# Top-k attention and a mixture of depths on one core: the bound rounded by ScalarE, fillers of two tiles at once, the mixture in even pieces, and four unread bf16 products ahead of each first turning

## The chip, the cores and the metric

The kernel runs on one core of one Trainium2 chip. The metric is the time of one execution on the device, in microseconds. The engines are TensorE (PE in the profile, its weight loads PEld), VectorE (DVE), ScalarE (ACT), GpSimd (POOL) and SyncE (SP, which here only issues transfers). A difference of more than about 0.2% can be told from none.

## The reference

Batch 8, 8 heads, 576 tokens, head width 64, all in float32. Attention keeps the 32 largest scores of each row; then, per batch, 128 tokens of the 512-wide result go through a two-layer network of width 1024.

```python
scores = scale * np.matmul(q, k.transpose(0, 1, 3, 2))     # scale = 1/8
kth = np.partition(scores, -32, axis=-1)[..., -32:-31]
scores = np.where(scores >= kth, scores, -1e9)
attn = softmax(scores)
x = np.matmul(attn, v)             # (B,H,S,D) -> (B,S,H*D)
s = x @ w_gate                     # per batch
top_idx = np.argpartition(-s[b], 128)[:128]
ye = np.maximum(x[b, top_idx] @ w1, 0) @ w2
out[b, top_idx] = x[b, top_idx] + sigmoid(s[b, top_idx])[:, None] * ye
```

## The kernel before

Work is cut into units (batch b, row tile t, head pair hp). Row tiles t = 0 to 3 have 128 rows and give two score tiles of 128 x 576, one for each head; row tile 4 has 64 rows, and its two heads share one score tile. So a batch has 20 units, 16 of two tiles and 4 of one. A loop over n runs a pipeline in which one pass (a step) works on six units at once, and every engine's instructions stay in the order of the program text (`InOrder`):

- n+1: `multiply` makes the scores (tile ps) on TensorE; at the end of the step `keep` copies them to sc on ScalarE.
- n: `find_bound` on VectorE. Each row is cut into eight parts, the eight largest of each are candidates, and three rounds of maximum give the 24th largest candidate (tile best), a bound below which the 32nd largest score is near. `cut` writes it, rounded to bf16, to `seen[:, 0]`.
- n-1: `part` on ScalarE takes the Sign of each score against the bound (tile sides) and counts the signs in `seen[:, 2]`. `mask` on GpSimd multiplies the scores by the signs into y and appends eight columns of fillers, made from that count so that the eighth largest of y is the wanted 32nd score. `find_kth` on VectorE takes the eight largest (next8), and `lift` on GpSimd writes the eighth, times 2^90, to `seen[:, 1]`.
- n-2: Relu on ScalarE and a subtraction on GpSimd push all scores below the 32nd far down (tile z).
- n-3: `turn` and `turn_last` transpose z on TensorE (tiles ptr, last_ps), ScalarE takes the exponential (pT, last).
- n-4: `values` multiplies by v on TensorE (tile av), `keep_values` copies to xs. After the fourth head pair of a row tile, `normalise` divides on VectorE and GpSimd (tile x), and `gates` multiplies by w_gate on VectorE.

`mixture` is a generator; each step runs one piece of it, after a batch's last tile has its gates. Its ten pieces: two transposes of the gates, two of ranks on VectorE, the picks, the gather of picked tokens (xe_ps), a small product for row numbers and gates, two halves of the first layer (h_ps), and the second layer (y_ps), whose result gy goes out by a GpSimd transfer. `load_qkv` is a generator too: in steps 10 to 18 of a batch it loads and transposes the next batch's keys and queries and loads its values. Its transposes, the mixture and `turn_last` share one PSUM buffer (`ps_misc`); the turnings have two (`ps_tr`), the scores one set, the values one. Keys, queries and values have two buffers, the fetched rows three. The end of the program checks the assumptions behind the bound, and a general path stands behind that check; it is not run with this input.

In the profile nearly every instruction carries line 41, that of the helper that keeps the order, so groups are told apart by tile.

Of the kernel before, what the change touches and what calls it, by code (L numbers as in the profile page):

```python
# [9 lines left out]
AF = mybir.ActivationFunctionType  # L10
ALU = mybir.AluOpType
FP32 = mybir.dt.float32
# [7 lines left out]

BIG = 2.0**90

TALL = 2.0**20


LEAST = 1.0e-16
MOST = 1.0e6


# [15 lines left out]
def kernel(  # L45
# [21 lines left out]
    DE = D + 1  # L67
    NDC = HD // P
    NFC = F // P
    scale = 1.0 / float(D) ** 0.5  # L70
    assert D == 64 and R == 64 and HD == 512 and F % (4 * P) == 0
    assert moe_capacity == CAP and TOP_K % 8 == 0

# [16 lines left out]
    ident = const.tile([P, P], FP32, name="ident")  # L90
    make_identity(nc, ident)


    tok_i = const.tile([P, NT], I32, name="tok_i")
    nc.gpsimd.iota(tok_i[:, 0:J], pattern=[[1, J]], base=0, channel_multiplier=J)
# [12 lines left out]
    nc.gpsimd.memset(sums, 1.0)  # L108

    MIDDLE = S - 2 * (TOP_K - 8) + 1  # L110
    steps_i = const.tile([P, 8], I32, name="steps_i")
    nc.gpsimd.iota(steps_i, pattern=[[2, 8]], base=2 - MIDDLE, channel_multiplier=0)
    steps = const.tile([P, 8], FP32, name="steps")
    nc.vector.tensor_copy(out=steps, in_=steps_i)


# [40 lines left out]
        qT = kqpool.tile([P, NHP, S], FP32, name="qT")  # L157
        return kT, qT, vbufs[b % 2]

    def load_qkv(qb, kb, vb, kT, qT, vs):  # L160

        last = [ldpool.tile([R, H, D], FP32, name=f"last{i}", bufs=1) for i in range(2)]
        for rows, src in zip(last, (kb, qb)):
            nc.sync.dma_start(out=rows, in_=src[:, JP:S, :].rearrange("h p d -> p h d"))

        def fetch(i):
            hp, src = i // 2, (kb, qb)[i % 2]
            rows = ldpool.tile([P, J, 2, D], FP32, name="rows")
            for hh in range(2):
                nc.sync.dma_start(  # L170
                    out=rows[:, :, hh, :],
                    in_=src[2 * hp + hh, 0:JP, :].rearrange("(p j) d -> p j d", j=J),
                )
            return rows

        fetched = [fetch(i) for i in range(3)]
        vt, vlast, vpair = vs
        v_rows = vb[:, JP:S, :].rearrange("h p d -> p h d")
        nc.sync.dma_start(out=vlast[:, :, 0:D], in_=v_rows)
        for hh in range(2):  # L180
            nc.sync.dma_start(
                out=vpair[hh * R : (hh + 1) * R, :, hh, 0:D], in_=v_rows[:, hh::2, :]
            )
        tr = ps_misc.tile([P, 512], FP32, name="tr", tag="misc")
        for i in range(2 * NHP):
            w, hp = divmod(i, NHP)
            pe.transpose(
                tr[:, i * R : (i + 1) * R],
                last[w][:, 2 * hp : 2 * hp + 2, :].rearrange("p h d -> p (h d)"),
                ident[0:R, 0:R],  # L190
            )
        tails = tr.rearrange("p (w c r) -> p w c r", w=2, c=NHP)
        act.copy(out=kT[:, :, 0:R], in_=tails[:, 0, :, :])
        act.copy(out=kT[:, :, S : S + R], in_=tails[:, 0, :, :])
        act.copy(out=qT[:, :, JP:S], in_=tails[:, 1, :, :])
        yield
        for i in range(2 * NHP):
            tr = ps_misc.tile([P, 512], FP32, name="tr", tag="misc")
            for c in range(J):
                pe.transpose(  # L200
                    tr[:, c * P : (c + 1) * P],
                    fetched[i][:, c, :, :].rearrange("p h d -> p (h d)"),
                    ident,
                )
            if i % 2 == 0:
                act.copy(out=kT[:, i // 2, R:S], in_=tr)
            else:
                act.copy(out=qT[:, i // 2, 0:JP], in_=tr)
            if i + 3 < 2 * NHP:
                fetched.append(fetch(i + 3))  # L210
            nc.sync.dma_start(
                out=vt[:, i, :, 0:D],
                in_=vb[i, 0:JP, :].rearrange("(p j) d -> p j d", j=J),
            )
            yield

    def heads_of(t):

# [55 lines left out]

    def cut(n, best, at):

        pool.tensor_copy(
            out=seen[:, 0, at : at + n],
            in_=best.rearrange("p i e -> p (i e)").bitcast(BF16)[:, 15 : 16 * n : 16],
        )  # L280
# [13 lines left out]
            accum_out=seen[:, 2, at + i : at + i + 1],  # L294
        )

    def mask(i, sc, at, sides, y):

        pool.tensor_tensor(y[:, i, 0:S], sc[:, i, :], sides[:, i, :], ALU.mult)
        pool.tensor_scalar(  # L300
            out=y[:, i, S : S + 8],
            in0=steps,
            scalar1=seen[:, 2, at + i : at + i + 1],
            scalar2=-TALL,
            op0=ALU.add,
            op1=ALU.mult,
        )

    def find_kth(n, y):
# [9 lines left out]
    def turn(i, z):  # L319

        tr = ps_tr.tile([P, 512], FP32, name="ptr")
        for c in range(J):
            at = c * P + i * R
            pe.transpose(tr[:, c * P : (c + 1) * P], z[:, i, at : at + P], ident)
        return tr
# [135 lines left out]
    def mixture(row0, x, gate, rank, exact=False):  # L461
# [31 lines left out]
                    op0=ALU.is_equal,  # L493
                )

        yield
        ps = ps_misc.tile([P, 512], FP32, name="xe_ps", tag="misc")
        for dc in range(NDC):
            for t in range(NT):
                n = R if t == J else P  # L500
                pe.matmul(
                    ps[:, dc * CAP : (dc + 1) * CAP],
                    x[0:n, t, dc * P : (dc + 1) * P],
                    pick[0:n, t, :],
                    start=(t == 0),
                    stop=(t == J),
                )
        xeT = modpool.tile([P, NDC, CAP], FP32, name="xeT")
        act.copy(out=xeT, in_=ps.rearrange("p (c i) -> p c i", c=NDC))

        yield
        ps = ps_misc.tile([P, 512], FP32, name="extra_ps", tag="misc")
# [13 lines left out]
        dve.tensor_scalar_min(out=row_i, in0=picked[:, 0:1], scalar1=float(B * S - 1))  # L526

        hT = modpool.tile([P, NFC, CAP], FP32, name="hT")
        for f0 in range(0, NFC, 4):
            yield  # L530
            ps = ps_misc.tile([P, 512], FP32, name="h_ps", tag="misc")
            for i in range(4):
                for dc in range(NDC):
                    pe.matmul(
                        ps[:, i * CAP : (i + 1) * CAP],
                        w1[:, dc, (f0 + i) * P : (f0 + i + 1) * P],
                        xeT[:, dc, :],
                        start=(dc == 0),
                        stop=(dc == NDC - 1),
                    )  # L540
            act.activation(
                hT[:, f0 : f0 + 4, :], ps.rearrange("p (c i) -> p c i", c=4), AF.Relu
            )

        yield
        ps = ps_misc.tile([P, 512], FP32, name="y_ps", tag="misc")
        for fc in range(NFC):
            pe.matmul(
                ps, hT[:, fc, :], w2[:, fc, :], start=(fc == 0), stop=(fc == NFC - 1)
            )  # L550
        gy = modpool.tile([P, HD], FP32, name="gy")
        act.activation(gy, ps, AF.Copy, scale=picked[:, 1:2])

        nc.gpsimd.indirect_dma_start(
            out=out.flatten_outer_dims(),
# [29 lines left out]

    units = [(b, t, hp) for b in range(B) for t in range(NT) for hp in range(NHP)]
    per_batch = NT * NHP
    load_from = per_batch - 2 - 2 * NHP
    first_tile, tiles = [], 0
    for b, t, hp in units:  # L590
        first_tile.append(tiles)
        tiles += len(heads_of(t))
    qkv = {0: room_for_qkv(0)}
    loading = load_qkv(q[0], k[0], v[0], *qkv[0])
    next(loading)
    mixing = iter(())
    gating = normalising = None
    xs = x = gate = None
# [4 lines left out]

    for n in range(-1, len(units) + 6):
        if 0 <= n + 1 < NHP:
            next(loading)
            next(loading)
        if n == NHP:
            load_weights()

# [24 lines left out]
        if tiles_of(n - 1):  # L635
            sides = wkpool.tile([P, 2, S], BF16, name="sides")
            y = wkpool.tile([P, 2, S + 8], FP32, name="y")
            for i in range(tiles_of(n - 1)):
                part(i, scs[n - 1], first_tile[n - 1], sides)
                mask(i, scs[n - 1], first_tile[n - 1], sides, y)  # L640
            next8 = find_kth(tiles_of(n - 1), y)
        if tiles_of(n - 3):
            w = tiles_of(n - 3)
# [27 lines left out]
        if tiles_of(n - 4):  # L671
# [5 lines left out]
                    gate = xpool.tile([P, NT], FP32, name="gate")  # L677
            weights.pop(n - 4)
            keep_values(t, hp, av, xs)
        if gating is not None:  # L680
            b, t, *of_batch = gating
            gating = None
# [11 lines left out]
        if tiles_of(n - 4):  # L694
            b, t, hp = units[n - 4]
            if hp == NHP - 1:
                normalising = b, t, xs, x, gate
        if tiles_of(n):
            cut(tiles_of(n), bests.pop(n), first_tile[n])
        if tiles_of(n - 1):  # L700
            lift(tiles_of(n - 1), next8, first_tile[n - 1])
        b, i = divmod(n, per_batch)
        if n >= 0 and i >= load_from and b + 1 < B:
            if i == load_from:
                qkv[b + 1] = room_for_qkv(b + 1)
                loading = load_qkv(q[b + 1], k[b + 1], v[b + 1], *qkv[b + 1])
            next(loading, None)

    for _ in mixing:
        pass  # L710
# [4 lines left out]
    for what, op, than, limit in (  # L715
        (seen[:, 0, :], ALU.min, ALU.is_gt, LEAST),
        (seen[:, 1, :], ALU.min, ALU.is_gt, LEAST * BIG),
        (seen[:, 2, :], ALU.max, ALU.is_lt, float(MIDDLE)),
        (seen[:, 2, :], ALU.min, ALU.is_gt, float(MIDDLE - 16)),
        (sums.rearrange("p t h -> p (t h)"), ALU.max, ALU.is_lt, MOST),  # L720
    ):
        far = stats.tile([P, 1], FP32, name="far")
# [51 lines left out]
    def general(b, row0):  # L774
# [1 line left out]
            return a[bass.ds(b, 1)].rearrange("o a s d -> (o a) s d")  # L776

        kT, qT, vs = room_for_qkv(0)
        for _ in load_qkv(of(q), of(k), of(v), kT, qT, vs):
            pass  # L780
        x = xpool.tile([P, NT, HD], FP32, name="x")
        gate = xpool.tile([P, NT], FP32, name="gate")
        for t in range(NT):
# [64 lines left out]
```

## Time and profile before

| | |
|---|---|
| median of 3 runs | 1368.69 us (1368.59 to 1369.9) |
| profiled execution | 1366.38 us, of which the span is 1364.4 |
| granted TensorE clock, mean | 0.823 |
| busy: PE, PEld | 1111.4 us (81%), 885.7 (65%) |
| busy: DVE, ACT, POOL | 910.9 (67%), 853.6 (63%), 983.1 (72%) |
| DMA | 46.92 MB, 33 GB/s over the span |

The span runs from the first to the last instruction. The busy shares are averages over steps of different kinds; which engine ends last is read step by step. The granted clock is a share of full speed.

### The profile page before, as it was taken

How to read it: one execution, taken by the hardware profiler on the slowest of the kernel's cores; microseconds unless marked ns; L12 is line 12 of the kernel's file. 1: busy time of each engine (PE TensorE's matmuls, PEld its weight loads, DVE VectorE, ACT ScalarE, POOL GpSimd, SP SyncE). 2: the span in 40 equal slices, each digit the busy share in tenths (PEclk: the TensorE clock that was granted, in tenths of full speed). 3: DMA queues.
4: the chain of work that ended last, by engine and by line, in shares of the span. 5: the costliest groups of instructions: out<-in, count | busy, mean ns of one | idle time of the engine just before them, and what ended most of it. 6: DMA issues, size and time to landing. Idle time of an engine off the chain costs nothing. (4 is left out here: it accounts for less than half of the span.)

```text
span 1364.4 us, 23293 instructions
## 1 busy us (share of the span) xinstructions
PE 1111.4 (81%) x6938; PEld 885.7 (65%) x6938; DVE 910.9 (67%) x4978; ACT 853.6 (63%) x1921; POOL 983.1 (72%) x1254
## 2 busy tenths in 40 slices
PE   4778866987879879898788986788886988879867
PEld 2566645865668657686567765676665866658655
DVE  3777678657785587855777658864778647786440
ACT  3677676656665667565675576765666566666530
POOL 3888788677775777667786678865788567887730
PEclk9678888988678886888777888879858799779768
DMA  8501120113001120012200122001210010000000
GB/s 189 120 4 37 44 62 1 25 33 81 16 2 24 39 77 14 2 31 40 78 6 8 24 50 68 6 16 32 58 48 1 9 40 32 5 1 2 8 35 10
DMA packets 123189, 46.92 MB, mean 34 GB/s; under 512 B 118832, under 2 KB 118832, under 8 KB 122032
## 3 DMA queue, kind: packets, MB, share of 16 engines
q1 hardware_dynamic: 121904, 43.27, 13.0%
q0 software_dynamic: 1152, 2.10, 1.2%
q8 instruction: 57, 0.93, 0.3%
q14 instruction: 76, 0.62, 0.1%
HBM read 33.82 MB, written 11.53 MB: 33 GB/s over the span
## 5 line engine op out<-in xcount | busy, mean ns | idle before, releaser
L41 POOL TENSOR_TENSOR y<-sc,sides 128x576 f32<-128x576 f32 x288 | 368.8, 1281 | 226.6 <-ACT sides L41 216.3
L41 POOL TENSOR_TENSOR z<-sc,z 128x576 f32<-128x576 f32 x288 | 413.3, 1454 | 21.3 <-ACT z L41 10.2
L41 DVE MAX8 next<-y 128x8 f32<-128x584 f32 x288 | 219.5, 766 | 306.3 <-POOL y L41 305.7
L41 PE MATMUL av<-v,pT 128*128 128x65 f32 (+1 forms) x2560 | 379.8, 304 | 13.2 <-ACT xs L41 13.2
L41 PEld LDWEIGHTS av<-v,pT 128*128 128x128 f32 (+1 forms) x2560 | 362.1, 223 | 32.2 <-ACT xs L41 25.0
L41 DVE MAX8 cand<-sc 128x8 f32<-128x72 f32 x2304 | 324.0, 217 | 86.0 <-ACT sc L41 86.0
L41 PE MATMUL ptr<-ident,z 128*128 128x128 f32 x1152 | 227.7, 331 | 178.2 <-POOL z L41 177.7
L41 ACT ACTIVATE sides<-sc,seen 128x576 bf16<-128x576 f32 x288 | 221.6, 772 | 153.0 <-POOL seen L41 152.0
L41 PEld LDWEIGHTS ptr<-ident,z 128*128 128x128 f32 x1152 | 160.8, 174 | 233.9 <-POOL z L41 228.0
L41 PE MATMUL ps<-kT,qT 64*128 64x288 f32 (+1 forms) x1280 | 252.2, 524 | 2.7 <-ACT qT L41 2.7
L41 ACT COPY sc<-ps 128x576 f32<-128x576 f32 x288 | 171.7, 646 | 122.1 <-issue 91.7
L41 ACT ACTIVATE z<-sc,seen 128x576 f32<-128x576 f32 x288 | 209.3, 777 | 0.6 <-POOL seen L41 0.6
L41 ACT ACTIVATE pT<-ptr 128x512 f32<-128x512 f32 x288 | 158.5, 584 | 18.9 <-PE ptr L41 18.6
L41 PEld LDWEIGHTS ps<-kT,qT 64*128 64x128 f32 (+1 forms) x1280 | 128.2, 218 | 57.8 <-issue 13.7
L41 DVE MAX8 best<-cand 128x8 f32<-128x64 f32 x864 | 154.6, 216 | 3.3
L41 DVE MATCH_REPLACE8 cand<-best,cand 128x64 f32<-128x64 f32 x576 | 116.5, 209 | 0.0
L41 POOL TENSOR_SCALAR y<-steps,seen 128x8 f32<-128x8 f32 x288 | 78.6, 273 | 22.6
L41 PE MATMUL tr<-ident,rows 128*128 128x128 f32 x256 | 48.5, 319 | 29.0 <-ACT hT L41 8.3
L41 PE MATMUL av<-vpair,last 128*128 128x130 f32 x256 | 68.8, 357 | 0.0
L41 PEld LDWEIGHTS tr<-ident,rows 128*128 128x128 f32 x256 | 31.0, 158 | 58.1 <-issue 16.1
L41 PEld LDWEIGHTS h_ps<-xeT,w 128*128 128x128 f32 x512 | 60.8, 198 | 8.7 <-issue 3.6
L41 PE MATMUL h_ps<-xeT,w 128*128 128x128 f32 x512 | 63.8, 285 | 1.2 <-ACT hT L41 0.7
(73 smaller groups left out, 959.4 us busy)
## 6 DMA issues: line engine op xcount, KB each, us to landing
rows<-in_k_dram SPq DMA_DIRECT2D x64, 128.0 KB, 2.8
rows<-in_q_dram SPq DMA_DIRECT2D x64, 128.0 KB, 2.7
v<-in_v_dram SPq DMA_DIRECT2D x64, 128.0 KB, 2.9
out_dram<-x SPq DMA_DIRECT2D x8, 1024.0 KB, 4.6
w<-in_moe_w_dram SPq DMA_DIRECT2D x2, 2048.0 KB, 11.1
last<-in_k_dram SPq DMA_DIRECT2D x8, 128.0 KB, 3.1
last<-in_q_dram SPq DMA_DIRECT2D x8, 128.0 KB, 3.3
vlast<-in_v_dram SPq DMA_DIRECT2D x8, 128.0 KB, 3.0
```

Source lines behind the costliest of these rows:

```text
L41: return lambda *a, **kw: self._tc.keep_in_program_order(fn(*a, **kw))
```

## The change

- Queries are multiplied by 2^-20 when they are copied after their transposes, and the exponential's scale by 2^20. Scores are then so small that plain whole numbers can serve as fillers: the factor TALL goes.
- `cut` moves from GpSimd to ScalarE, and to another place in the step: right behind `keep_values`, ahead of the gates, the mixture's piece and the normalising.
- The fillers of both tiles are written by one GpSimd instruction (`fill`), behind both products y, in place of one for each tile.
- `turn` of a step's first tile issues four bf16 products of 128 x 128 by 128 x 512 into the turning's PSUM buffer, which the turnings then overwrite. Nobody reads them.
- The mixture has 16 pieces in place of 10: the gather in four, the first layer in four, the second in two.
- The loader is split. Keys and queries of the next batch are loaded and transposed in steps 0 to 8 (in the first batch 4 to 12), the values in one go in step 6 (the first batch's at n = -1).
- One more check at the end (the smallest sum).

```diff
-    scale = 1.0 / float(D) ** 0.5
+    scale = 1.0 / float(D) ** 0.5 / SMALLER
+    busy = const.tile([P, 512], BF16, name="busy")
+    nc.gpsimd.memset(busy, 1.0)
...
-        act.copy(out=qT[:, :, JP:S], in_=tails[:, 1, :, :])
+        act.mul(out=qT[:, :, JP:S], in_=tails[:, 1, :, :], mul=SMALLER)
...
-                act.copy(out=qT[:, i // 2, 0:JP], in_=tr)
+                act.mul(out=qT[:, i // 2, 0:JP], in_=tr, mul=SMALLER)
...
-        pool.tensor_copy(
+        act.copy(
             out=seen[:, 0, at : at + n],
...
-    def mask(i, sc, at, sides, y):
-        pool.tensor_tensor(y[:, i, 0:S], sc[:, i, :], sides[:, i, :], ALU.mult)
-        pool.tensor_scalar(
-            out=y[:, i, S : S + 8],
-            in0=steps,
-            scalar1=seen[:, 2, at + i : at + i + 1],
-            scalar2=-TALL,
+    def fill(n, y, at):
+        pool.tensor_tensor(
+            y[:, 0:n, S : S + 8],
+            steps[:, 0:n, :],
+            seen[:, 2, at : at + n].unsqueeze(2).to_broadcast([P, n, 8]),
+            ALU.subtract,
...
         tr = ps_tr.tile([P, 512], FP32, name="ptr")
+        for _ in range(4 if i == 0 else 0):
+            pe.matmul(tr, busy[:, 0:P], busy)
...
-        yield
-        ps = ps_misc.tile([P, 512], FP32, name="xe_ps", tag="misc")
         for dc in range(NDC):
+            yield
+            ps = ps_misc.tile([P, 512], FP32, name="xe_ps", tag="misc")
...
-        act.copy(out=xeT, in_=ps.rearrange("p (c i) -> p c i", c=NDC))
+            act.copy(out=xeT[:, dc, :], in_=ps[:, 0:CAP])
...
-        for f0 in range(0, NFC, 4):
+        for f0 in range(0, NFC, 2):
...
+        for half in (slice(0, HD // 2), slice(HD // 2, HD)):
+            yield
+            ps = ps_misc.tile([P, 512], FP32, name="y_ps", tag="misc")
+            for fc in range(NFC):
+                pe.matmul(ps[:, 0 : HD // 2], hT[:, fc, :], w2[:, fc, half], ...)
+            act.activation(gy[:, half], ps[:, 0 : HD // 2], AF.Copy, scale=picked[:, 1:2])
...
+            fill(tiles_of(n - 1), y, first_tile[n - 1])
...
+        if tiles_of(n):
+            cut(tiles_of(n), bests.pop(n), first_tile[n])
         if gating is not None:
...
-        if tiles_of(n):
-            cut(tiles_of(n), bests.pop(n), first_tile[n])
...
-        if n >= 0 and i >= load_from and b + 1 < B:
-            if i == load_from:
+        if n >= 0 and b + 1 < B:
+            if n == NHP if b == 0 else i == 0:
                 qkv[b + 1] = room_for_qkv(b + 1)
-                loading = load_qkv(q[b + 1], k[b + 1], v[b + 1], *qkv[b + 1])
-            next(loading, None)
+                loading = load_kq(k[b + 1], q[b + 1], *qkv[b + 1][0:2])
+            if i == v_at:
+                load_v(v[b + 1], qkv[b + 1][2])
+            if n >= NHP:
+                next(loading, None)
```

## Rows read from the trace of the kernel before

**Rows 1.** The cores: span and mean granted clock.
```profile
core 0: 1364.4 us, clock 0.823
```
**Rows 2.** The waits, summed: total us, times, longest.
```profile
PE ptr L41 <- POOL z L41: 177.7, 103, 4.6
...
ACT sides L41 <- POOL seen L41: 152.0, 96, 3.4
...
POOL out_dram L554 <- ACT gy L41: 66.6, 8, 35.6
...
PE tr L41 <- DMA rows<-in_q_dram: 7.2, 1, 7.2
```
**Rows 3.** Timeline of GpSimd in a plain step: start, duration, instruction, idle before.
```profile
376.39 1.28 POOL L41 TENSOR_TENSOR y<-sc,sides 128x576 f32<-128x576 f32 x1 [0.67 <-ACT sides L41]
377.75 0.27 POOL L41 TENSOR_SCALAR y<-steps,seen 128x8 f32<-128x8 f32 x1
378.10 1.28 POOL L41 TENSOR_TENSOR y<-sc,sides 128x576 f32<-128x576 f32 x1
...
382.53 0.19 POOL L41 CAST seen<-best 128x2 f32<-128x2 bf16 x1
382.82 0.22 POOL L41 TENSOR_SCALAR seen<-next 128x2 f32<-128x2 f32 x1
383.71 1.28 POOL L41 TENSOR_TENSOR y<-sc,sides 128x576 f32<-128x576 f32 x1 [0.67 <-ACT sides L41]
```
**Rows 4.** Timeline of ScalarE in the same step.
```profile
375.44 0.78 ACT L41 ACTIVATE sides<-sc,seen 128x576 bf16<-128x576 f32 x1 [1.87 <-POOL seen L41]
...
380.47 0.29 ACT L41 COPY xs<-av 128x130 f32<-128x130 f32 x1
382.76 0.78 ACT L41 ACTIVATE sides<-sc,seen 128x576 bf16<-128x576 f32 x1 [2.00 <-POOL seen L41]
```
**Rows 5.** Timeline of TensorE in the same step.
```profile
377.14 1.24 PE L41 MATMUL ps<-kT,qT 64*128 64x288 f32 x8
381.28 0.66 PE L41 MATMUL ptr<-ident,z 128*128 128x128 f32 x4 [2.90 <-POOL z L41]
```
**Rows 6.** Windows: length, busy us (instructions) by engine, clock, DMA share, GB/s.
```profile
164.48:1303.74 1139.26, 951.81 (x6017) 761.70 (x6018) 792.88 (x4337) 738.78 (x1669) 853.88 (x1077) 0.83 0.12 28
375.44:382.76 7.32, 4.42 (x37) 3.74 (x37) 5.18 (x21) 5.32 (x12) 6.24 (x8) 1.00 0.01 2
542.07:550.05 7.98, 7.71 (x33) 6.04 (x32) 5.85 (x26) 5.42 (x12) 6.45 (x9) 0.50 0.00 1
494.93:558.92 63.99, 55.31 (x274) 43.27 (x272) 49.28 (x270) 42.41 (x95) 51.41 (x65) 0.60 0.12 34
558.92:568.29 9.37, 7.16 (x58) 6.33 (x58) 8.47 (x41) 5.75 (x16) 6.91 (x9) 1.00 0.00 1
568.29:622.78 54.49, 49.48 (x319) 40.00 (x318) 32.67 (x198) 32.30 (x73) 34.11 (x41) 0.91 0.09 21
622.78:659.67 36.89, 30.52 (x222) 23.63 (x220) 23.33 (x115) 26.06 (x60) 29.58 (x39) 0.91 0.26 54
644.55:648.87 4.32, 3.58 (x28) 2.58 (x29) 2.43 (x12) 3.96 (x9) 3.32 (x5) 1.00 0.02 3
```
**Rows 7.** Groups of instructions: busy us, mean ns of one, idle before.
```profile
L41 POOL TENSOR_TENSOR x<-xs,rden 128x512 f32<-128x512 f32 (+1 forms) x40 | 41.7, 1044 | 13.7 <-DVE rden L41 13.7
L41 POOL CAST seen<-best 128x2 f32<-128x2 bf16 (+1 forms) x160 | 37.0, 231 | 9.2 <-DVE best L41 9.2
...
L41 ACT COPY picked<-extra_ps 128x2 f32<-128x2 f32 x8 | 1.7, 217 | 1.5 <-PE extra_ps L41 1.5
```
**Rows 8.** Timeline of TensorE: large mixture pieces at full clock.
```profile
571.07 6.08 PE L41 MATMUL xe_ps<-pick,x 128*128 128x128 f32 x40 [1.45 <-ACT last L41]
...
1344.70 3.84 PE L41 MATMUL h_ps<-xeT,w 128*128 128x128 f32 x32 [0.69 <-ACT hT L41]
1349.23 7.13 PE L41 MATMUL y_ps<-w,hT 128*128 128x512 f32 x16 [0.69 <-ACT hT L41]
```

More of the change, by code (lines that the diff above doesn't have):

```diff
@@ L21 @@
 BIG = 2.0**90
-TALL = 2.0**20
-LEAST = 1.0e-16
+SMALLER = 2.0**-20
+LEAST = 1.0e-16 * SMALLER
+FEWEST = 0.5
 MOST = 1.0e6
@@ L110 @@
     MIDDLE = S - 2 * (TOP_K - 8) + 1
-    steps_i = const.tile([P, 8], I32, name="steps_i")
-    nc.gpsimd.iota(steps_i, pattern=[[2, 8]], base=2 - MIDDLE, channel_multiplier=0)
-    steps = const.tile([P, 8], FP32, name="steps")
+    steps_i = const.tile([P, 2, 8], I32, name="steps_i")
+    nc.gpsimd.iota(
+        steps_i, pattern=[[0, 2], [-2, 8]], base=MIDDLE - 2, channel_multiplier=0
+    )
+    steps = const.tile([P, 2, 8], FP32, name="steps")
     nc.vector.tensor_copy(out=steps, in_=steps_i)
@@ L158, in room_for_qkv, with load_kq @@
         return kT, qT, vbufs[b % 2]
-    def load_qkv(qb, kb, vb, kT, qT, vs):
+    def load_kq(kb, qb, kT, qT):
         last = [ldpool.tile([R, H, D], FP32, name=f"last{i}", bufs=1) for i in range(2)]
@@ L176, in load_qkv @@
         fetched = [fetch(i) for i in range(3)]
[L177 to L183, printed above, removed]
         tr = ps_misc.tile([P, 512], FP32, name="tr", tag="misc")
@@ L207, in load_qkv, with load_v @@
             else:
-                act.copy(out=qT[:, i // 2, 0:JP], in_=tr)
+                act.mul(out=qT[:, i // 2, 0:JP], in_=tr, mul=SMALLER)
             if i + 3 < 2 * NHP:
                 fetched.append(fetch(i + 3))
+            yield
+    def load_v(vb, vs):
+        vt, vlast, vpair = vs
+        v_rows = vb[:, JP:S, :].rearrange("h p d -> p h d")
+        nc.sync.dma_start(out=vlast[:, :, 0:D], in_=v_rows)
+        for hh in range(2):
             nc.sync.dma_start(
-                out=vt[:, i, :, 0:D],
-                in_=vb[i, 0:JP, :].rearrange("(p j) d -> p j d", j=J),
-            )
-            yield
+                out=vpair[hh * R : (hh + 1) * R, :, hh, 0:D], in_=v_rows[:, hh::2, :]
+            )
+        for h in range(H):
+            nc.sync.dma_start(
+                out=vt[:, h, :, 0:D],
+                in_=vb[h, 0:JP, :].rearrange("(p j) d -> p j d", j=J),
+            )
     def heads_of(t):
@@ L295, in part @@
         )
-    def mask(i, sc, at, sides, y):
-        pool.tensor_tensor(y[:, i, 0:S], sc[:, i, :], sides[:, i, :], ALU.mult)
-        pool.tensor_scalar(
-            out=y[:, i, S : S + 8],
-            in0=steps,
-            scalar1=seen[:, 2, at + i : at + i + 1],
-            scalar2=-TALL,
-            op0=ALU.add,
-            op1=ALU.mult,
+    def fill(n, y, at):
[4 more added lines that the diff above has]
+            ALU.subtract,
         )
@@ L494, in mixture @@
                 )
-        yield
-        ps = ps_misc.tile([P, 512], FP32, name="xe_ps", tag="misc")
+        xeT = modpool.tile([P, NDC, CAP], FP32, name="xeT")
         for dc in range(NDC):
+            yield
+            ps = ps_misc.tile([P, 512], FP32, name="xe_ps", tag="misc")
             for t in range(NT):
@@ L501, in mixture @@
                 pe.matmul(
-                    ps[:, dc * CAP : (dc + 1) * CAP],
+                    ps[:, 0:CAP],
                     x[0:n, t, dc * P : (dc + 1) * P],
@@ L507, in mixture @@
                 )
-        xeT = modpool.tile([P, NDC, CAP], FP32, name="xeT")
-        act.copy(out=xeT, in_=ps.rearrange("p (c i) -> p c i", c=NDC))
+            act.copy(out=xeT[:, dc, :], in_=ps[:, 0:CAP])
         yield
@@ L528, in mixture @@
         hT = modpool.tile([P, NFC, CAP], FP32, name="hT")
-        for f0 in range(0, NFC, 4):
+        for f0 in range(0, NFC, 2):
             yield
             ps = ps_misc.tile([P, 512], FP32, name="h_ps", tag="misc")
-            for i in range(4):
+            for i in range(2):
                 for dc in range(NDC):
@@ L541, in mixture @@
             act.activation(
[L542 to L549, printed above, removed]
+                hT[:, f0 : f0 + 2, :],
+                ps[:, 0 : 2 * CAP].rearrange("p (c i) -> p c i", c=2),
+                AF.Relu,
             )
         gy = modpool.tile([P, HD], FP32, name="gy")
-        act.activation(gy, ps, AF.Copy, scale=picked[:, 1:2])
+        for half in (slice(0, HD // 2), slice(HD // 2, HD)):
+            yield
+            ps = ps_misc.tile([P, 512], FP32, name="y_ps", tag="misc")
+            for fc in range(NFC):
+                pe.matmul(
+                    ps[:, 0 : HD // 2],
+                    hT[:, fc, :],
+                    w2[:, fc, half],
+                    start=(fc == 0),
+                    stop=(fc == NFC - 1),
+                )
+            act.activation(
+                gy[:, half], ps[:, 0 : HD // 2], AF.Copy, scale=picked[:, 1:2]
+            )
         nc.gpsimd.indirect_dma_start(
@@ L587 @@
     per_batch = NT * NHP
-    load_from = per_batch - 2 - 2 * NHP
+    v_at = 6
     first_tile, tiles = [], 0
@@ L593 @@
     qkv = {0: room_for_qkv(0)}
-    loading = load_qkv(q[0], k[0], v[0], *qkv[0])
-    next(loading)
+    first_load = load_kq(k[0], q[0], *qkv[0][0:2])
+    next(first_load)
     mixing = iter(())
@@ L605 @@
         if 0 <= n + 1 < NHP:
-            next(loading)
-            next(loading)
+            next(first_load)
+            next(first_load)
+        if n == -1:
+            load_v(v[0], qkv[0][2])
         if n == NHP:
@@ L639 @@
                 part(i, scs[n - 1], first_tile[n - 1], sides)
-                mask(i, scs[n - 1], first_tile[n - 1], sides, y)
+                pool.tensor_tensor(
+                    y[:, i, 0:S], scs[n - 1][:, i, :], sides[:, i, :], ALU.mult
+                )
+            fill(tiles_of(n - 1), y, first_tile[n - 1])
             next8 = find_kth(tiles_of(n - 1), y)
@@ L719 @@
         (seen[:, 2, :], ALU.min, ALU.is_gt, float(MIDDLE - 16)),
+        (sums.rearrange("p t h -> p (t h)"), ALU.min, ALU.is_gt, FEWEST),
         (sums.rearrange("p t h -> p (t h)"), ALU.max, ALU.is_lt, MOST),
@@ L778, in general @@
         kT, qT, vs = room_for_qkv(0)
-        for _ in load_qkv(of(q), of(k), of(v), kT, qT, vs):
+        for _ in load_kq(of(k), of(q), kT, qT):
             pass
+        load_v(of(v), vs)
         x = xpool.tile([P, NT, HD], FP32, name="x")
```

## The prediction

> **What bounds the kernel now.** First the clock of the core [rows 1]: 0.823 on average. TensorE has two levels, 2.4 and 1.2 GHz, so a mean of 0.823 means that about 35% of the span ran at the lower one (0.65 x 1 + 0.35 x 0.5 = 0.825). Second the waits [rows 2]: TensorE's turnings wait for GpSimd's z, and ScalarE's Sign (`part`, tile sides) waits 152 us for GpSimd's `seen`. These point at a loop through GpSimd and ScalarE. Third the timelines of one plain two-tile step at full clock, begun by its first Sign at 375.44 and ended by the next step's at 382.76, 7.32 us. On GpSimd [rows 3] the order is y, filler, y, filler, z, z, `cut` (CAST), `lift`. `cut` starts at 382.53 and the next y only at 383.71, 1.18 us later, although cut and lift together take under 0.6: y waits 0.67 for the Sign, and the Sign had to wait for `cut`. On ScalarE [rows 4] the last work of the step begins at 380.47 and takes 0.29; then it stands still for 2.00 us until `cut` has been done. On TensorE [rows 5] the score products start at 377.14 for 1.24 us, and the first turning waits 2.90 us for z. The busy times of that step [rows 6] are PE 4.42, DVE 5.18, ACT 5.32, POOL 6.24 of 7.32. So at full clock GpSimd and the Sign behind `cut` set the step. At the low level, in the step at 542.07, PE is busy 7.71 of 7.98 us [rows 6] and sets it itself. The third kind of step is one with a large piece of the mixture: 568.29 to 622.78 holds five steps and takes 54.49 us, with PE busy 49.48 [rows 6].
>
> I number the steps of a batch by n mod 20, so that step 1 is the one after n = 20. The batch between 494.93 and 659.67 is steps 1 to 20 and takes 164.74; between 164.48 and 1303.74 seven batches take 1139.26, or 162.8 each [rows 6].
>
> **Part 1: `cut` to ScalarE, `fill` once for two tiles.** Of the 1.18 us between the start of `cut` and the next y, only `lift` remains, 0.28 with its gap: 0.90 less. One filler goes, 0.35 from its start to the next y's [rows 3]; the one left writes 16 columns and reads two tensors, which no row shows. Bounds: 0.27, as for 8 columns, and 1.28, as a 576-column product. It is nearest the first; I allow 0.08 more. A plain step becomes 7.32 - 0.90 - 0.35 + 0.08 = 6.15. On ScalarE `cut` costs between the 0.217 of its two-column copy and GpSimd's 0.231 [rows 7], hidden in the 2.00 idle us: 5.32 + 0.22 = 5.5 of 6.15. It waits there for VectorE's third maximum, with the mixture's copies, the loader's and the next Sign queued behind it. VectorE starts on a bound when ScalarE has copied the scores, at the end of the step before; its whole step is 5.2 us, the maxima of y still to come, while ScalarE has 5.3 of its own ahead of `cut` [rows 6]. So the bound is ready first, and only steps with extra VectorE work make it late. `fill` now comes behind both y, so `find_kth` of the first tile starts some 1.6 us later; its answer is wanted by `lift` behind both z, still later. The scaling of qT and of the exponential adds no instruction. Should each of the 40 scaled copies take a further 0.78 (a whole Sign [rows 4]), that is 31 us of ScalarE spread under its slack; I take nothing.
>
> **Part 2: the four bf16 products.** No row shows a bf16 product. An f32 product with 512 columns takes two records of 7.13 / 16 = 0.45 us at full clock [rows 8]. Bounds for four bf16 products: nothing on the path (they fit into PE's wait of 2.90, or into the 6.15 - 4.42 = 1.73 left of it), and 4 x 0.45 = 1.8 us if one costs a record. With half the bytes I take half a record, 0.22 each, 0.9 in sum. PE then has 4.42 + 0.9 = 5.3 of 6.15 to do. In a plain step that is hidden; in a step where the mixture keeps PE busy it is paid whole. In exchange PE's long wait, after which the clock falls, is mostly gone: I expect the full level for nearly all of a batch. What stands for this: the half step at 644.55 held 1.00 with PE busy 3.58 of 4.32, 83% [rows 6], and 5.3 of 6.15 is 86%. What the clock costs now is read from steps 1 to 8: 63.99, where eight plain steps and two normalising products of 1.04 [rows 7] would be 8 x 7.32 + 2.08 = 60.6, so 3.4 per batch and 24 over seven. The Trainium skill (TensorE: Matmul & The Clock Gate, Part 1) says that the loss to ramping is under 1% of a usual kernel's span, which here would be at most 14 us; the sum would end at 1245 instead of 1235. The mean of 0.823 speaks for the larger loss.
>
> **Part 3: the mixture in even pieces.** Its 10 pieces become 16, one per step from 5 on. From [rows 8]: the gather 6.08 in four, 1.52 each; w1 3.84 x 2 in four, 1.92 each; w2 7.13 in two, 3.57 each. These now fall on steps 10 to 13, 15 to 18, and 19 and 20; the loader moves from steps 10 to 18 to steps 0 to 8. Per step the longest engine counts:
> Steps 1 to 8: 5.6 (first, half a step in z), 6.3 three times (6.15 and 0.15 for the loader), 7.3 twice (with the normalising product), 7.0 (VectorE's gate product), 7.9 (VectorE ranks three columns): 54.0, now 63.99.
> Step 9, VectorE and ScalarE in turn for the picks: 9.5, now 9.37.
> Steps 10 to 14: PE 5.3 + 1.52 = 6.9, 6.9, then 7.3 (normalising), 7.2 (gate product), 6.6: 34.9, now 54.49.
> Steps 15 to 20: PE has half the score products in 15 to 18, so 6.7, 7.3, 6.9, 6.7; then 8.6 for about 4.1 + 0.9 + 3.57; then 9.5 for 3.6 + 0.9 + 3.57 = 8.1 and 1.4 of GpSimd's wait for gy, which now takes (66.6 - 35.6) / 7 = 4.4 each time [rows 2]: 45.7, now 36.89.
> Sum 144.1. Over seven batches 7 x 144.1 = 1009 against 1139: 130 saved.
>
> **Ends.** In the first batch 13 plain full steps save 1.16 each, 15; from this I take one wait for a landing of 7.2 [rows 2], since the value loads, the weights and the next batch's keys stand in a new order on SP's queue: 8. At the end the last mixture runs alone; six more pieces each cost a round through ScalarE of 0.69 [rows 8], 4. One more memset and one more check: 1. In all 130 + 8 - 5 = 133. The profiled execution took 1366.4, of which 1364.4 was span; its outside of 2 us stays. 1366.4 - 133 = 1233; the median of the runs stands 2.3 above the profiled one, so **1235**.
>
> **Rivals.**
> A, the other side: the products don't lift the clock. A plain step at the low level is PE's: 7.71 and four products at double price, 1.8, so 9.5 or more against 6.2: 3.3 lost each time. The gain of 133 is 16.6 per batch, so five low steps among the 16 full ones of a batch eat it; the present share, 35%, is 5.7, which gives 1366 + 8 x 0.7 x 3.3, about 1387. For it: at 542.07 PE was 97% busy and still stood at 0.50 [rows 6], so being busy alone does not raise the level. Against it: the products fill the very wait that keeps PE idle now. The Trainium skill (TensorE: Matmul & The Clock Gate, Part 4) says that turnings do not count as busy for the clock; that row, in which turnings are part of the busy time, agrees.
> B: the products cost a record each, 1.8. PE has 6.2 in a plain step and is the bound everywhere; the some 12 steps per batch with mixture or loader pay 0.9 more: 8 x 12 x 0.9 = 86, so 1320.
> C: `cut` makes ScalarE wait for VectorE. If it comes 0.5 late in each of 160 steps, with everything behind it, 80 us: 1315. For it: VectorE is at 8.47 of 9.37 in step 9 [rows 6]. Against it: what ScalarE has ahead of it, as above.
> D: the pieces and the wait for gy hide more than I allow, and a step with a piece ends near 6.3: 10 us less per batch, 1160.
>
> **Chances and range.** My sum 0.60 (1190 to 1275), A 0.09, B 0.11, C 0.10, D 0.10. The range of 1160 to 1320 takes in the sum with B and C nearly whole and the near half of D. A change of 0.2% is about what this kernel's runs can tell from none: A's price straddles it, so slower 0.07, same 0.02, faster 0.91.
>
> **What would show it.** The granted clock near 0.95 or above; plain steps of 6.1 to 6.3 us; GpSimd's y following `lift` with no wait for the Sign, and the total of ScalarE's waits for `seen` far below 152; a wait of ScalarE's `cut` for VectorE of under 0.5 us in most steps; bf16 products of about 0.22 us; steps 10 to 14 at about 35 us and steps 15 to 20 longer than now. It is wrong if low-clock steps remain (A), if PE is busy to the end in plain steps (B), or if ScalarE waits for VectorE at every `cut` (C).

## The result and the profile after

The changed kernel takes 1187.08 us (median of 4 runs, 1184.93 to 1189.01) against 1369.3 for the kernel before in the same comparison. The ratio is 0.8653, 95% interval 0.8605 to 0.870: faster by 13.5%. The forecast was 1235, range 1160 to 1320; the gain was 182 us where 134 were forecast. One trace below, of the kernel with the rounding back on GpSimd, is of a run in a slower state (1271.99 us, where the other four runs of that kernel took 1248 to 1251).

The cores and the waits of the changed kernel (total us, times, longest):
```profile
core 0: 1183.5 us, clock 0.954
```
```profile
POOL y L42 <- ACT sides L42: 133.5, 76, 22.0
...
ACT sc L42 <- PE ps L42: 64.9, 102, 2.4
...
PE ptr L42 <- POOL z L42: 46.5, 38, 3.8
```
The same wait of GpSimd's y for the Sign in the kernel before:
```profile
POOL y L41 <- ACT sides L41: 216.3, 160, 11.8
```
The mean clock went from 0.823 [rows 1] to 0.954. TensorE's wait for z fell from 177.7 to 46.5, and the Sign's wait for GpSimd's `seen` (152.0 in [rows 2]) is gone from the list. ScalarE's largest wait is now for TensorE's scores. GpSimd's y still waits for the Sign, 133.5 us where it was 216.3.

Step 8 of a batch, from the Sign at 471.62 to the next at 477.39, on GpSimd, ScalarE and TensorE. It has two tiles and runs a loader piece, and VectorE also ranks tokens for the mixture in it. These lines answer to [rows 3], [rows 4] and [rows 5]:
```profile
471.86 0.22 POOL L42 TENSOR_SCALAR seen<-next 128x2 f32<-128x2 f32 x1
472.66 2.53 POOL L42 TENSOR_TENSOR y<-sc,sides 128x576 f32<-128x576 f32 x2 [0.59 <-ACT sides L42]
475.14 0.23 POOL L42 TENSOR_TENSOR y<-steps,seen 128x16 f32<-128x16 f32 x1
475.31 2.79 POOL L42 TENSOR_TENSOR z<-sc,z 128x576 f32<-128x576 f32 x2
```
```profile
471.62 0.81 ACT L42 ACTIVATE sides<-sc,seen 128x576 bf16<-128x576 f32 x1
...
476.80 0.27 ACT L42 CAST seen<-best 128x2 f32<-128x2 bf16 x1
476.90 0.67 ACT L42 ACTIVATE qT<-tr 128x512 f32<-128x512 f32 x1
477.39 0.85 ACT L42 ACTIVATE sides<-sc,seen 128x576 bf16<-128x576 f32 x1
```
```profile
474.10 1.24 PE L42 MATMUL ps<-kT,qT 64*128 64x288 f32 x8
475.27 0.66 PE L42 MATMUL tr<-ident,rows 128*128 128x128 f32 x4
475.77 1.03 PE L42 MATMUL ptr<-busy 128*128 128x512 bf16 x4
476.78 0.66 PE L42 MATMUL ptr<-ident,z 128*128 128x128 f32 x4
```
The step takes 5.77 us where the plain step of [rows 4] took 7.32. ScalarE goes from `cut` through the loader's copy to the next Sign without a gap. On TensorE the loader's turnings and the bf16 products fill what was a wait of 2.90 us for z [rows 5]. So both engines are busy throughout; the first experiment tells which of them sets such a step. On GpSimd two y and their filler go from 472.66 to the z at 475.31, 2.65 us, 1.33 a tile; before, one tile's y and filler took from 376.39 to 378.10, 1.71 [rows 3]. Its first y still waits 0.59 for the Sign.

Windows of the changed kernel, in the columns of [rows 6]: the same 140 steps as from 164.48 to 1303.74 in the kernel before; step 8 from above; step 4 of the same batch; then its steps 1 to 8, 9, 10 to 14 and 15 to 20:
```profile
143.24:1113.00 969.76, 907.65 (x6671) 714.70 (x6672) 774.34 (x4335) 759.69 (x1849) 775.42 (x825) 0.97 0.14 33
...
471.62:477.39 5.77, 5.77 (x46) 4.44 (x45) 5.73 (x36) 5.77 (x16) 5.10 (x7) 1.00 0.21 47
445.12:450.88 5.76, 5.68 (x44) 4.33 (x43) 4.82 (x27) 5.76 (x15) 5.47 (x7) 1.00 0.18 38
427.51:477.39 49.88, 45.48 (x354) 34.38 (x353) 42.78 (x238) 46.16 (x113) 46.33 (x50) 1.00 0.40 91
477.39:489.15 11.76, 8.47 (x55) 7.12 (x53) 10.71 (x51) 5.91 (x16) 7.92 (x9) 0.80 0.10 23
489.15:522.00 32.85, 32.85 (x227) 26.33 (x227) 28.44 (x167) 28.76 (x71) 29.06 (x30) 0.92 0.01 1
522.00:567.85 45.85, 45.28 (x337) 36.39 (x336) 28.64 (x165) 28.62 (x72) 27.74 (x33) 1.00 0.04 10
```
PE is busy without a gap through steps 10 to 14 and nearly so to step 20: TensorE sets these steps, 78.7 us of the batch. In steps 1 to 8 PE, ACT and POOL are each busy 45 to 46 of 49.88 us, and no one engine sets them all. GpSimd, the bound before, has 3 to 18 us to spare in the four groups. They add up to 140.3 us (before, 164.7).

### The profile page after: what moved, and what is told of

Read it like the earlier page. It is cut to its first block, busy times and chain, and to the rows that moved or that the text cites. A ratio compares the mean times of both kernels' runs of the same rounds, so it can differ in the third digit from the quotient of the medians.

```text
span 1183.5 us, 24519 instructions
## 1 busy us (share of the span) xinstructions
PE 1072.9 (91%) x7706; PEld 838.0 (71%) x7706; DVE 893.6 (76%) x4980; ACT 878.5 (74%) x2129; POOL 895.9 (76%) x967
## 3 DMA queue, kind: packets, MB, share of 16 engines
q8 instruction: 63, 1.03, 0.3%
## 4 chain that ended last, share of the span: by engine, by line
PE 64%; ACT 15%; POOL 12%; issue 4%; DVE 3%; SPq 1%; DMA 1%; POOLq 0%; ACTq 0%
PE av L42 19%; PE ptr L42 16%; PE ps L42 11%; POOL y L42 6%; PE h_ps L42 6%; PE xe_ps L42 5%; PE y_ps L42 5%; POOL z L42 5%; ACT sc L42 3%; ACT sides L42 3%; ACT z L42 3%; ACT pT L42 2%; PE tr L42 2%; PE last_ps L42 1%; POOL out_dram L572 1%
## 5 line engine op out<-in xcount | busy, mean ns | idle before, releaser
L42 POOL TENSOR_TENSOR y<-sc,sides 128x576 f32<-128x576 f32 x288 | 363.7, 1282 | 140.2 <-ACT sides L42 133.5
L42 POOL TENSOR_TENSOR z<-sc,z 128x576 f32<-128x576 f32 x288 | 401.2, 1413 | 28.0 <-ACT z L42 25.8
L42 PE MATMUL av<-v,pT 128*128 128x65 f32 (+1 forms) x2560 | 308.6, 265 | 0.4 <-ACT xs L42 0.4
L42 PEld LDWEIGHTS av<-v,pT 128*128 128x128 f32 (+1 forms) x2560 | 292.2, 186 | 9.1 <-issue 3.8
L42 PE MATMUL ptr<-ident,z 128*128 128x128 f32 x1152 | 185.0, 285 | 47.0 <-POOL z L42 46.5
L42 PE MATMUL ps<-kT,qT 64*128 64x288 f32 (+1 forms) x1280 | 207.3, 444 | 2.7 <-ACT qT L42 2.7
L42 PEld LDWEIGHTS ptr<-ident,z 128*128 128x128 f32 x1152 | 137.2, 148 | 96.6 <-POOL z L42 76.5
L42 PE MATMUL ptr<-busy 128*128 128x512 bf16 x640 | 166.6, 383 | 0.0
L42 PEld LDWEIGHTS ps<-kT,qT 64*128 64x128 f32 (+1 forms) x1280 | 108.2, 183 | 44.2 <-ACT qT L42 4.3
L42 PEld LDWEIGHTS <-busy 128*128 128x128 bf16 x640 | 57.5, 98 | 54.4 <-issue 10.8
L572 POOL DMA_INDIRECT out_dram<-gy,row_i x8 | 13.0, 1629 | 73.2 <-ACT gy L42 73.2
```

The source lines that it names most:

```text
L42: return lambda *a, **kw: self._tc.keep_in_program_order(fn(*a, **kw))
L572: nc.gpsimd.indirect_dma_start(out=out.flatten_outer_dims(), out_offset=bass.IndirectOffsetOnAxis(ap=row_i, axis=0), in_=gy, in_offset=Non ...
```

## Experiments

All are kernels timed over three rounds against the kernel before, which took 1369 to 1373 us in them. Runs of one kernel lie up to 1.4% apart (1171.13 to 1187.92 without the products), more than the 0.2% taken ahead of the prediction, so differences of a few us are not read.

**Without the products.**
```diff
-        for _ in range(4 if i == 0 else 0):
+        for _ in range(0):
             pe.matmul(tr, busy[:, 0:P], busy)
```


> The changed kernel without the four bf16 products, all else kept. My theory (the products buy the clock, at about 1.0 us of TensorE per step): the granted clock falls from 0.954 to about 0.85, and the time goes up to about 1230 us (1205 to 1260), because steps at the low level take 8 us and more, although steps at full clock with a mixture piece get shorter by up to 1 us. Rival (the shorter step keeps TensorE busy enough by itself, and the products only cost): the clock stays above 0.93 and the time falls to about 1100 us (1080 to 1150).


Measured: 1183.35 us, ratio 0.8623 (0.8559 to 0.8688), clock 0.894. Neither came. In time the four products are worth nothing in this kernel, though they change the clock. A step 4 with TensorE's first turning of it, then a step 6 and a step 16:
```profile
442.63:448.39 5.76, 4.83 (x40) 3.98 (x39) 4.71 (x26) 5.76 (x15) 5.46 (x7) 1.00 0.15 33
...
447.77 0.66 PE L42 MATMUL ptr<-ident,z 128*128 128x128 f32 x4 [0.93 <-POOL z L42]
...
593.24:603.21 9.97, 8.42 (x41) 7.21 (x40) 8.93 (x54) 6.25 (x17) 6.89 (x8) 0.52 0.13 28
666.52:672.57 6.05, 6.05 (x54) 5.28 (x53) 3.90 (x13) 5.14 (x14) 5.71 (x7) 1.00 0.00 0
```
Step 4 takes 5.76 us as it does with the products. TensorE is busy only 4.83 of them and waits 0.93 for z, while ScalarE is busy throughout: ScalarE sets this kind of step, and the products are free in it. Step 16 keeps the full level by the mixture's own work and takes 6.05 in place of 6.91. Step 6 takes 9.5 to 10 us, at the low level for most of it, in three of seven batches (9.97 in the one shown) and 6.77 in the other four; with products it takes 7.31. Cost and gain cancel.

**The products alone.** The kernel before with the memset of `busy` and the loop of four products in `turn`, nothing else.


> The kernel before with the four bf16 products and nothing else of the change. My theory (in its plain step they fit into the wait of 2.9 us and hold the clock): clock 0.93 or more, about 1345 us (1325 to 1360), a gain of the 24 us that low-level steps cost, a little eaten by steps with a mixture piece, which pay about 1 us each. Rival 1 (they do not lift the clock, low steps pay double): 1390 us or more at about 0.82. Rival 2 (they are most of the whole gain): under 1300 us.


Measured: 1347.54 us, ratio 0.9827 (0.9796 to 0.9858), clock 0.898 in its profile: 23.5 us less. The time is as my theory had it; the clock is lower than it expected. TensorE in a plain step of that kernel:
```profile
511.45 1.04 PE L41 MATMUL ptr<-busy 128*128 128x512 bf16 x4
514.58 0.66 PE L41 MATMUL ptr<-ident,z 128*128 128x128 f32 x4 [2.09 <-POOL z L41]
```
The products lie inside the wait for z, of which 2.09 us remain.

**The rounding back on GpSimd.** `cut` by `pool.tensor_copy`, and its call moved back to the place ahead of `lift`.


> The changed kernel with the rounding of the bound back on GpSimd and back at its old place in the step, behind the normalising product and the mixture's transfer. My theory (the loop of GpSimd and the Sign gets 0.9 us longer, which counts where TensorE does not set the step): plain steps of 6.4 to 6.7 in place of 5.8, steps 10 to 18 nearly unchanged, 1187 plus 6 to 8 us per batch, about 1240 us (1220 to 1260). Rival (TensorE sets every step now, so where the rounding runs is no matter): 1187 within 8 us.


Measured: 1250.15 us, ratio 0.9122 (0.9094 to 0.9151): 63 us more than the changed kernel, near the theory. The Signs of a step 15 at full granted clock, 6.55 apart, and GpSimd at the end of that step:
```profile
567.71 0.78 ACT L42 ACTIVATE sides<-sc,seen 128x576 bf16<-128x576 f32 x1 [1.16 <-POOL seen L42]
...
574.26 0.78 ACT L42 ACTIVATE sides<-sc,seen 128x576 bf16<-128x576 f32 x1 [1.26 <-POOL seen L42]
```
```profile
574.04 0.19 POOL L42 CAST seen<-best 128x2 f32<-128x2 bf16 x1
574.31 0.22 POOL L42 TENSOR_SCALAR seen<-next 128x2 f32<-128x2 f32 x1
575.21 1.28 POOL L42 TENSOR_TENSOR y<-sc,sides 128x576 f32<-128x576 f32 x1 [0.68 <-ACT sides L42]
```
It is the picture of [rows 3] again: the Sign waits 1.26 us for `seen`, and 1.17 us pass from the rounding to the next y, 0.68 of it a wait for the Sign. TensorE is busy 6.50 us in this step, which has a piece of the mixture. But step 3 of the batch, which has none and keeps TensorE busy 5.8, takes 6.55 too: it is the loop that keeps the Signs apart.

**The mixture in its ten old pieces.** The gather, both halves of the first layer and the second layer as in the kernel before.


> The changed kernel with the mixture in its ten old pieces. My theory (a large piece is paid whole in its step, and steps without a piece fall back to GpSimd's 5.7 us and cannot use the time saved on TensorE): steps of 11 to 13 us with the gather or the second layer, about 4 to 8 us more per batch, about 1225 us (1210 to 1260). Rival (TensorE sets every step, so its work costs the same wherever it lies): 1187 within 8 us.


Measured: 1197.18 us, ratio 0.874 (0.8713 to 0.8766): 10 us more. The even pieces are worth about a quarter of what my theory gave them, and the rival is nearer. Steps 10 to 14 and 15 to 20 of one batch:
```profile
495.94:541.46 45.52, 43.20 (x291) 33.53 (x295) 32.19 (x198) 29.96 (x71) 29.39 (x30) 1.00 0.00 1
541.46:575.74 34.28, 31.19 (x239) 23.05 (x240) 23.04 (x113) 26.42 (x65) 28.76 (x32) 1.00 0.13 23
```
The five steps take 45.52 and the six behind them 34.28, 79.8 in sum, against 32.85 + 45.85 = 78.7 in even pieces. TensorE's work is merely moved.

**Products only where no piece runs.**
```diff
-                trs.append(turn(i, z))
+                trs.append(turn(i, z, 4 if 2 <= n % 20 <= 10 else 0))
```


> The changed kernel with the four products only in steps 2 to 10 of each batch, where no piece of the mixture occupies TensorE; steps 11 to 20 go without. My theory (the products cost about 0.8 us in each step with a piece, where the clock stays up without them, and buy the clock in the other steps): clock 0.94 or more, steps 11 to 18 as without products (5.8 to 6.1), steps 2 to 10 as with them, about 1130 us (1110 to 1155). Rival (the products in the steps with pieces also hold the clock of the steps behind them): the clock falls to about 0.90 and the time stays at 1180 or above.


Measured: 1168.76 us, ratio 0.8527 (0.8503 to 0.8551), clock 0.927. Neither came. Steps 11 to 13 and 16 to 18 fell to 5.8 and 6.05, as my theory had it, but step 15 went to 10. Steps 14 and 15:
```profile
510.00:516.99 6.99, 5.71 (x45) 5.00 (x45) 6.99 (x35) 5.79 (x16) 6.83 (x7) 1.00 0.00 0
516.99:526.96 9.97, 9.80 (x56) 8.21 (x57) 7.98 (x47) 5.38 (x15) 7.34 (x9) 0.66 0.01 2
```
The piece of step 14 is the small product for row numbers; TensorE was busy 5.71 of its 6.99 us, and step 15 ran mostly at the low level, in all seven batches with a mixture to run. Without any products it did so in three of the seven, so what precedes the fall is not settled by this.

**Two products in place of four.** `range(2 if i == 0 else 0)`.


> The changed kernel with two products in place of four. My theory (cost and gain of the products balance over the whole kernel, so half of them gives half of each): clock between 0.894 and 0.954, time 1170 to 1190 us. Rival (there is a number from which on the clock holds, and two are below it): the clock as without them, 0.89 to 0.90, and 1185 us or more.


Measured: 1162.96 us, ratio 0.8479 (0.8436 to 0.8521), clock 0.938. Better than either expected. Cost and gain are not in proportion: over their four runs each, two products hold 0.938 to 0.959, four 0.947 to 0.956 and none 0.885 to 0.911. Two keep the clock about as well as four, and save 24 us against four.

**The rounding on ScalarE alone**, in the kernel before, at the changed kernel's place.


> The kernel before with nothing but the rounding of the bound on ScalarE, at the place of the changed kernel. My theory (this wait is the largest part of the change): plain steps at full clock of 6.4 us in place of 7.3, about 75 us less, 1295 us (1275 to 1320). Rival (without the fillers and the spread pieces it frees GpSimd only for other waits): 1340 us or more.


Measured: 1304.62 us, ratio 0.952 (0.9494 to 0.9547): 64 us less, near the theory. Its clock is 0.847. A full-level step, in which ScalarE is busy throughout, and a low one, in which TensorE is busy 9.26 of 10.31:
```profile
501.32:507.08 5.76, 4.46 (x35) 3.61 (x35) 5.04 (x28) 5.76 (x15) 4.64 (x6) 1.00 0.10 23
520.20:530.51 10.31, 9.26 (x40) 7.60 (x40) 9.94 (x50) 5.76 (x14) 9.00 (x10) 0.52 0.01 2
```

**A filler for each tile**, of 8 columns, right behind its y, in the changed kernel's form (one subtraction with a broadcast count).


> The changed kernel with one filler instruction for each tile, directly behind that tile's product, as before (each writes 8 columns). My theory (TensorE at 5.7 us sets the plain step, and GpSimd, at 5.6 to 5.7, is close behind): GpSimd goes to about 6.0, which costs 0.2 to 0.3 us in steps 2 to 9, 1187 plus about 15, 1195 to 1210 us. Rival (GpSimd has slack everywhere): 1187 within 6 us.


Measured: 1187.37 us, ratio 0.8662 (0.8638 to 0.8687): no difference. My theory falls, and GpSimd shows why it did not get slower:
```profile
472.58 1.28 POOL L42 TENSOR_TENSOR y<-sc,sides 128x576 f32<-128x576 f32 x1 [0.45 <-ACT sides L42]
473.82 0.20 POOL L42 TENSOR_TENSOR y<-steps,seen 128x8 f32<-128x8 f32 x1
473.98 1.28 POOL L42 TENSOR_TENSOR y<-sc,sides 128x576 f32<-128x576 f32 x1
```
One tile takes 1.40 (472.58 to 473.98) against 1.71 before [rows 3]. So it is the new form of the filler that saves GpSimd 0.31 a tile; writing two at once saves 0.07 more (1.33), and GpSimd has that to spare.

**Two products, only in steps 2 to 10, 14 and 15.**
```diff
+                trs.append(turn(i, z, 2 if n % 20 in (2, 3, 4, 5, 6, 7, 8, 9, 10, 14, 15) else 0))
```


> The changed kernel with two products in steps 2 to 10, 14 and 15 of each batch, none in the others. My theory (with the products only in steps 2 to 10 the clock fell behind the small product of step 14, so that step 15 took 10.0 in place of 6.9; two products there hold it): step 15 at about 7, 3 us per batch less than with products in steps 2 to 10 alone, and the halved products give another 0.6 or so, about 1145 us (1130 to 1160). Rival (low stretches come back elsewhere): 1163 or more, as with two products everywhere.


Measured: 1149.64 us, ratio 0.8367 (0.8341 to 0.8393): as my theory had it, and 37 us less than the changed kernel. Step 15 holds the full level:
```profile
514.29:521.15 6.86, 6.86 (x58) 5.90 (x57) 6.86 (x42) 5.39 (x15) 6.70 (x8) 1.00 0.01 1
```

**The loader back at steps 10 to 18**, the values in step 12.
```diff
-            if n == NHP if b == 0 else i == 0:
+            if i == load_from:
...
-            if n >= NHP:
+            if i >= load_from:
                 next(loading, None)
```


> The changed kernel with the loader of the next batch's keys and queries back at steps 10 to 18 and its values in step 12. My theory (those steps are set by TensorE, to which each piece of the loader adds 0.5 us, while steps 2 to 9 gain less): 2 us more per batch, about 1200 us (1190 to 1220). Rival (its place is no matter): 1187 within 6 us.


Measured: 1250.93 us, ratio 0.9118 (0.9097 to 0.9139): 64 us more, as much as the rounding, and five times what I expected. Steps 16 to 18 take 8.05 in place of 6.91. A step 16 of this kernel with the end of it on TensorE and ScalarE, then the same of the changed kernel, which has the same work but for the loader:
```profile
554.37:562.43 8.06, 7.53 (x60) 6.19 (x60) 4.20 (x14) 5.98 (x16) 6.63 (x7) 1.00 0.14 33
...
558.72 2.05 PE L42 MATMUL h_ps<-xeT,w 128*128 128x128 f32 x16
561.24 0.66 PE L42 MATMUL tr<-ident,rows 128*128 128x128 f32 x4 [0.47 <-ACT hT L42]
...
560.80 0.38 ACT L42 ACTIVATE hT<-h_ps 128x256 f32<-128x256 f32 x1 [1.07 <-PE h_ps L42]
561.93 0.60 ACT L42 ACTIVATE qT<-tr 128x512 f32<-128x512 f32 x1 [0.75 <-PE tr L42]
562.43 0.77 ACT L42 ACTIVATE sides<-sc,seen 128x576 bf16<-128x576 f32 x1
```
```profile
529.11:536.02 6.91, 6.91 (x57) 5.70 (x56) 3.99 (x20) 5.37 (x14) 5.80 (x6) 1.00 0.00 0
...
533.65 2.05 PE L42 MATMUL h_ps<-xeT,w 128*128 128x128 f32 x16
...
535.74 0.39 ACT L42 ACTIVATE hT<-h_ps 128x256 f32<-128x256 f32 x1 [1.07 <-PE h_ps L42]
536.02 0.77 ACT L42 ACTIVATE sides<-sc,seen 128x576 bf16<-128x576 f32 x1
```
The mixture and the loader share one PSUM buffer. With both in a step, the loader's turnings wait for ScalarE to empty it (0.47 idle), ScalarE then waits for the turnings (0.75), and the next Sign stands behind their copy: 1.63 us from the Relu's start to the Sign in place of 0.28. Of the 1.15 us that the step is longer, 0.62 is the turnings' own work (TensorE busy 7.53 in place of 6.91) and 0.53 is TensorE standing still. My theory had the first, not the second. Nor did steps 1 to 8 gain anything by losing the loader: 52.43 us in one batch, at a clock of 0.93, where they take 49.88 with it, at 1.00. That the shared buffer makes the 0.53 is read from these lines; no run gave the loader a buffer of its own.

**The rounding on ScalarE at its old place in the step.**


> The changed kernel with the rounding still on ScalarE, but at its old place in the step, behind the mixture's piece and the normalising. My theory (on ScalarE only the next Sign follows either way, so the engine counts and not the place): 1187 within 6 us. Rival (behind the mixture's copies it waits for TensorE's pieces): 1200 us or more.


Measured: 1187.64 us, ratio 0.8655 (0.8635 to 0.8675). The engine counts, the place does not.

**Rounding and products together** in the kernel before.


> The kernel before with the rounding on ScalarE at the new place and the four products, without the joint filler, the pieces and the loader's move. My theory (the rounding shortens the step, the products then hold the clock): clock 0.94 or more, about 1215 us (1195 to 1235), that is, most of the whole gain. Rival (the gains of the two alone, 64 and 24 us, only add): about 1281 us.


Measured: 1282.12 us, ratio 0.9345 (0.9321 to 0.9368). The rival, within 1 us: the two gains only add, although the clock is 0.957.

## Why the prediction was right in its range and too high

The experiments split the 182 us in a chain of medians: the rounding 64 (1368.8 to 1304.6), the products on top 22 (to 1282.1), the filler and the loader's move together 85 (to 1197.2, the kernel with whole pieces), the even pieces 10 (to 1187.1). The split holds for this order, and to a few us, since the medians come from different rounds. Taken out of the changed kernel, the rounding is worth 63, the loader's move 64, the pieces 10 and the products nothing. No run takes the filler's new form back, so its share of the 85 is not measured.

**Part 1.** The loop of GpSimd and the Sign behind `cut` was the bound, and `cut` on ScalarE saves what was said. With the rounding put back the loop takes 6.55, and GpSimd's own work in the step shown without it is 2.65 + 2.79 + 0.22 = 5.66: 0.89, where 0.90 was taken. VectorE's maximum did not hold `cut` up (rival C did not come): the whole list of waits has one of 0.4 us for it. The scaled copies of the queries, which were taken at nothing, cost 0.63 each where the plain ones cost 0.60. The term that was mis-sized is the filler. I took 0.27 off a step (0.35 less, 0.08 more); two tiles went from 2 x 1.71 to 2.65, 0.77, because the new instruction form is cheaper, not because there is one fewer.

So GpSimd needs 5.66 where I had 6.15, and the next bound came into sight. I expected 5.5 us of ScalarE; with `cut` (0.10 from its start to the next) and the loader's copy (0.49) it is full at 5.77, and it sets such a step with the products or without. That is also why y still waits 0.59 for the Sign, where the prediction named a y without that wait as a sign of being right.

**Part 2.** The price of a product was right: 1.03 us for four at full level, and 0.86 from the first of them to the turning behind them in the step before the one shown. The 24 us put on the clock agree with the 23.5 that the products alone bring in the kernel before, but by luck. They were read from the batch whose steps 1 to 8 are the longest of seven (60.4 to 64.0, mean 62.2). With the products alone these steps take 60.5, as was worked out (60.6), so the clock cost them 1.6 us a batch, 11.5 over seven; the rest does not lie in these steps. The Trainium skill puts the loss to ramping at under 1% of a usual kernel's span (TensorE: Matmul & The Clock Gate, Part 1), by estimate 14 us here. In this kernel it is more: the 23.5 have the products' own cost already paid.

That the products would be a gain in the changed kernel as a whole was wrong. In steps 10 to 20 they are paid, as forecast, but I left out that those steps mostly keep the full level without them; in steps 1 to 8 they hold the level. By the traces' means steps 1 to 8 take 50.0 us with them and 52.6 without, steps 10 to 20 77.4 with and 73.7 without. Rival B, TensorE as the bound of every step, did not come: ScalarE sets steps such as 4 and 8, and four products cost 1.03 and not 1.8. Rival A did not come; the mean clock is 0.954.

**Part 3.** By groups, forecast and measured in the batch shown: steps 1 to 8 54.0 and 49.9; step 9 9.5 and 11.8; steps 10 to 14 34.9 and 32.85; steps 15 to 20 45.7 and 45.85; in sum 144.1 and 140.3. The sum was near, its reason was not. I credited the drop in steps 10 to 14 to the even pieces. They mostly move TensorE's work, and bring 10 us. What I gave 0.15 us a step, the loader, is worth 64: it left the steps that TensorE sets, where it cost its own work and, by the lines above, a queue behind the mixture for the shared PSUM buffer, and went to steps that did not get longer by it. In the trace before, TensorE's turnings of the loader and the gates (tr) waited for ScalarE's hT, gy, picked and xeT for 8.3, 4.7, 4.4 and 4.1 us, small waits that I passed over, and I did not ask what stood behind them. The first of them:
```profile
PE tr L41 <- ACT hT L41: 8.3, 12, 0.7
```
Step 9 was 2.3 worse. But no step took the 7.9 that I gave the ranks ahead of it, and steps 8 and 9 together take 17.53 where 7.9 + 9.5 = 17.4 were forecast, so the delay of the ranks came a step later and was not added:
```profile
479.96 1.04 POOL L42 TENSOR_TENSOR x<-xs,rden 128x512 f32<-128x512 f32 x1 [1.85 <-DVE rden L42]
481.07 0.21 POOL L42 TENSOR_SCALAR seen<-next 128x2 f32<-128x2 f32 x1
...
481.32 1.44 ACT L42 ACTIVATE z<-sc,seen 128x576 f32<-128x576 f32 x2 [1.09 <-POOL seen L42]
...
485.46 1.11 PE L42 MATMUL ptr<-ident,z 128*128 128x128 f32 x4 [3.29 <-POOL z L42]
```
In the changed kernel's step 9 VectorE, late from the ranks, holds GpSimd's x; `lift` stands behind x, the Relu behind `lift`, and TensorE waits 3.29 for z; the granted clock of step 9 is 0.80. This is read from the trace and was not tried.

**Ends and sum.** The 140 steps that were forecast at 1009 us take 969.8. The first batch up to them gained more than the 8 forecast (136.1 to 113.6 us, counted from the first Sign, which comes 1.3 later). The tail lost 9.8 (60.7 to 70.5) where 5 were forecast with the memset and the check; why it lost more was not tried.

## What to carry over

When one engine's loop is shortened, redo the sum for every other engine, in each kind of step: here ScalarE became the bound of some steps and TensorE of others. Unread products were free where TensorE waited and cost 0.86 us where it set the step, so give them only to the steps that need them, and no more than hold the clock. Two engines that are both full in a step do not tell which sets it; taking work off one does. Work that two producers put into one buffer in the same step can cost a round through the engine that empties it; moving one of them to other steps was worth more here than splitting the other's work. Take an edit apart by its instruction forms too: here "one filler for two tiles" saved GpSimd's time by the form, not by the count.

## What was not expected of the hardware

On GpSimd an 8-column filler by a two-input subtraction takes 0.16 us to the start of what follows it (473.82 to 473.98), where the scalar form took 0.35 (377.75 to 378.10 in [rows 3]), and it starts 0.12 sooner behind the product ahead of it (1.24 from the product's start against 1.36, though the product takes 1.28 in both). Why the forms differ is open. And the granted clock is no measure of a kernel's time: 0.894, 0.938 and 0.954 went with 1183, 1163 and 1187 us.
